# x^T U of the first two batches in plain float32: an attention and channel-mixing kernel on one core, with its steps in another order

## The chip, the cores and the metric

The kernel runs on one core of one Trainium2 chip. The metric is device time in microseconds: 933.13 us is the median of three runs of the kernel before (932.9 to 933.77). One profiled execution of it took 933.82 us; its trace spans 932.0 us. In the profile PE is TensorE (PEld its weight loads), DVE is VectorE, ACT is ScalarE, POOL is GpSimd and SP the engine that issues the transfers. A number like L449 is a line of the kernel.

## The reference

Linear attention with a norm for each head, then a low-rank mixing along the sequence and a feed-forward net, for 8 batches of 576 positions and 512 channels (8 heads of 64):

```python
kv = np.einsum('bhsd,bhse->bhde', k, v)
out = np.einsum('bhsd,bhde->bhse', q, kv)
rms = np.sqrt(np.mean(out * out, axis=-1, keepdims=True) + 1e-06)
x = (out / rms * g_norm)              # then heads side by side: [8, 576, 512]
...
xt = x.transpose(0, 2, 1)
h = xt @ U @ V                        # U: 576 x 32, V: 32 x 576
u = x + h.transpose(0, 2, 1)
ch = np.maximum(u @ w_ch1, 0.0) @ w_ch2   # 512 -> 2048 -> 512
y = u + ch
```

U, V and the two weights come as float64 bits, which the kernel turns into float32 on the chip with byte and bit operations.

## The kernel before, in words

**The feed-forward net** sets the frame. The 4608 rows (8 x 576) are cut into nine blocks of 512. For each block the 2048 hidden channels are taken in 16 chunks f of 128. A chunk is `ffn1` (L432 to L434: four column tiles d of 128 channels, three matmuls each), `relu` (ACT makes `hh`, L441, DVE makes `hl`, L442) and `ffn2` (L449: four output tiles, three matmuls each). The three matmuls are the two halves of a float32 split: a value is stored as a high part rounded to the type float32r and a low part, the rest, and high x high, low x high and high x low are added. So u is held as `uth` and `utl`, the hidden values as `hh` and `hl`, the weights as `ws` with two halves. `ffn2` of a chunk comes one chunk later, so that PE has `ffn1` of the next chunk to do while ACT and DVE make `hh` and `hl`.

**The preparation of a batch** goes in four pairs of heads. `kv` (L259, L263) makes the two 64x64 products into `kvb`; `out` (L282, L284) multiplies by q; ACT squares, DVE reduces (L298), ACT and DVE form the reciprocal root, DVE multiplies (L311, L313): x, with positions on partitions. Then x is split into `xh` (L142) and `xl` (L154, L327); `t_step` forms x^T U on PE with U in two parts (`u2`, 64 columns: high and low side by side; L354, L356), five matmuls with `xh` and four with `xl`; `t4_step` adds and splits the result into `t4`; `turn_step` transposes x on DVE (L339) and with 16 small transfers on SP (L342) into `ut32`; `mix_step` multiplies `t4` by V (L424), adds it to `ut32` (L426) and splits the sum into `uth` and `utl` (`split_cols`, L389, L390). From batch 2 on the last 64 positions of k and v are split too (`tails`, L254 to L256).

**Batch b+1 is prepared within block b.** A table, `STEPS`, gives the half chunk at which each pair's step is placed; batch 1 has its own, `STEPS0`, because block 0 also decodes the weights of its later chunks. The compiler's own scheduler may move an instruction from that place, by its model of time; what comes out is one fixed order on each engine.

**Batch 0 has nothing to hide behind.** Its steps, with the decoding of U, V and the first three chunks' weights, are named and listed by hand in `ORDER0`: `kv0`, `out0`, `sq0` (squares), `red0`, `ta0`/`hf0`/`rc0`/`nw0` (the root), `mul0`, `xh0`/`xl0`/`xt0` (the split of x), `tx0`/`txl0` (x^T U with the high and the low part of x: ten matmuls, L655, and four, L659), `t4c0`/`t4s0`, `tr0` (the transpose on PE, L650), `mix0` (L673), `uh0`/`ul0` (`uth` and `utl` of column tile 0), for pairs 0 to 3; `w1...`, `w2...`, `c...`, `e...` and `m...` are weights: A (copy of bytes, L128), D0 to D2 (DVE), B (merge, L129), H and L (the halves, L544 and L547). `f0a` to `f0d` are `ffn1` of chunk 0. The engines take their queues in that order. What of batch 0 does not fit in block 0, its last 64 positions, is done by `mix_rest` (L414, L416) at half steps 3, 5, 7 and 9 of block 0.

Slots of weights that come late serve as room for early data: `x123` (x of pairs 1 to 3) lies in weight 15's, `xhl0` (the split x of odd pairs) in 14's, `u4` (U in four parts) in 13's; a weight's load waits until its slot is free.

Of the kernel before, what the change touches and what calls it, by code (L numbers as in the profile page):

```python
# [58 lines left out]
def build(ctx: ExitStack, tc: tile.TileContext, kv_in, kvt0_in, kvt_in, q_in, uv_in, g_in, w_in, out):  # L59
# [285 lines left out]
    def t_step(b, p):  # L345
        xh, xl = state[b, p]["hl"]
        tp = bank()
        if b == 0:
            todo = [(u, xh, i) for u in u4 for i in range(NT)] + [(u4[0], xl, i) for i in range(4)]
            for n, (u, xx, i) in enumerate(todo):  # L350
                nc.tensor.matmul(tp[0:2 * R, 0:P], lhsT=u[:, i, :], rhs=xx[:, i, :], start=(n == 0), stop=(n == len(todo) - 1))
        else:
            for i in range(NT):
                nc.tensor.matmul(tp[0:2 * R, 0:P], lhsT=u2[:, i, :], rhs=xh[:, i, :], start=(i == 0), stop=(i == NT - 1))  # L354
                if i < 4:
                    nc.tensor.matmul(tp[0:2 * R, 0:P], lhsT=u2[:, i, :], rhs=xl[:, i, :], start=False, stop=False)  # L356
        state[b, p]["tp"] = tp

    def t4_step(b, p):
# [227 lines left out]
    step["u2v"] = lambda: nc.vector.tensor_copy(out=u2[:, :, 0:R], in_=u4[0][:, :, 0:R].bitcast(F32))  # L587
    step["u2a"] = lambda: nc.scalar.copy(out=u2[:, :, R:2 * R], in_=u4[1][:, :, 0:R].bitcast(F32))

    def first_pair(p):  # L590
# [16 lines left out]
        def kv():  # L607
# [29 lines left out]
        def x_high():  # L637
            own["xh"], own["xl"] = xhl0 if p % 2 else [sc.tile([P, n, P], F32R, name=s) for s, n in (("xh", NT), ("xl", 4))]
            nc.scalar.copy(out=own["xh"], in_=x)

        def x_low():
            nc.vector.tensor_tensor(out=own["xl"], in0=x[:, 0:4], in1=own["xh"][:, 0:4].bitcast(F32), op=ALU.subtract)

        def x_rest():
            xh = own["xh"]
            nc.vector.tensor_tensor(out=xh[TAIL:P, 4], in0=x[0:TAIL, 4], in1=xh[0:TAIL, 4].bitcast(F32), op=ALU.subtract)

# [8 lines left out]

        def t_low():
            for i in range(4):
                nc.tensor.matmul(tp, lhsT=u4[0][:, i, :], rhs=own["xl"][:, i, :], start=False, stop=(i == 3))  # L659
# [9 lines left out]
        def mix():  # L669
# [170 lines left out]
```

## Time and profile before

| | |
|---|---|
| median of 3 runs | 933.13 us (932.9 to 933.77) |
| the profiled execution | 933.82 us, its span 932.0 us |
| PE busy | 912.5 us, 98% of the span |
| DVE, ACT, POOL busy | 413.9, 280.5, 48.3 us |
| block 0, first FFN matmul | 30.30 us |
| block 1, first FFN matmul | 140.68 us |
| block 1, second chunk's first FFN matmul | 159.69 us |
| mean granted clock | 0.993 |

A busy PE may still be slow: the granted clock halves in some stretches, and a matmul's shown duration (0.39 us for 512 columns) is longer than its step from one to the next, since they overlap. So work is priced here by steps between starts.

### The profile page before, as it was taken

Reading aid. Unit: us, or ns where it says so; the run is one execution under the profiler, and the core shown is the slowest. Engines: PE = TensorE matmul, PEld = TensorE weight load, DVE = VectorE, ACT = ScalarE, POOL = GpSimd, SP = SyncE. Lnnn points to the kernel's source line nnn. Section 1 sums busy time; section 2 is a strip of 40 time slices with the busy share of each in tenths; the row PEclk is TensorE's granted clock in tenths of the full one; section 3 lists DMA queues with packets and bytes.
Section 4 is the critical chain, followed back from the end, with each engine's and each line's share of the span. In section 5 each row is a group of like instructions: output and inputs, shape, how many; then the busy total and the mean of one; then the engine's idle time right before and its main releaser. Section 6 shows DMA issues by size and latency. Waiting matters only on the chain.

```text
span 932.0 us, 12204 instructions
## 1 busy us (share of the span) xinstructions
PE 912.5 (98%) x4560; PEld 761.4 (82%) x4560; DVE 413.9 (44%) x890; ACT 280.5 (30%) x592; POOL 48.3 (5%) x66
## 2 busy tenths in 40 slices
PE   8899997999999999999999999999999999999998
PEld 7777886888888888888888888888788888888887
DVE  5889976444354345444244435434344331112112
ACT  6677753222223223222222222222222221111110
POOL 3000002000020002000200001000200020002000
PEclk9999997999999999999999999999999999999999
DMA  9951123321122121211122122212111010001001
GB/s 346 415 211 47 48 62 104 88 56 54 49 95 58 32 78 63 80 34 57 59 59 71 30 70 74 80 32 73 57 49 27 13 46 1 1 0 46 1 1 46
DMA packets 43019, 65.48 MB, mean 70 GB/s; under 512 B 9680, under 2 KB 27856, under 8 KB 42960
## 3 DMA queue, kind: packets, MB, share of 16 engines
q1 hardware_dynamic: 42960, 64.70, 21.2%
q8 instruction: 36, 0.59, 0.3%
q14 instruction: 23, 0.19, 0.1%
HBM read 46.97 MB, written 9.44 MB: 61 GB/s over the span
## 4 chain that ended last, share of the span: by engine, by line
PE 79%; DVE 1%; SPq 1%; DMA 1%; POOL 0%; issue 0%; DVEq 0%; POOLq 0%
PE y L449 36%; PE h L432 12%; PE h L433 12%; PE h L434 12%; PE pp L259 2%; PE pp L282 2%; SPq L342 1%; PE pp L354 1%; PE pp L449 1%; PE pp L356 1%; PE pp L424 1%; DVE utl L390 1%; PE pp L284 1%; DMA out<-st 0%; DVE st L460 0%; DMA kv_sb<-kv_in 0%
## 5 line engine op out<-in xcount | busy, mean ns | idle before, releaser
L449 PE MATMUL y<-hh,ws 128*128 128x512 f32 x1000 | 327.4, 394 | 2.9 <-ACT hh L441 2.9
L442 DVE SCALAR_TENSOR_TENSOR hl<-h,hh 128x512 fp32r<-128x512 f32 x143 | 98.6, 690 | 298.4 <-ACT hh L441 297.2
L449 PEld LDWEIGHTS y<-hh,ws 128*128 128x128 f32 x1000 | 180.8, 188 | 37.9 <-ACT hh L441 4.5
L441 ACT ACTIVATE hh<-h 128x512 fp32r<-128x512 f32 x143 | 85.3, 597 | 377.4 <-PE h L434 377.2
L432 PE MATMUL h<-uth,ws 128*128 128x512 f32 x500 | 197.1, 394 | 0.9 <-DVE hl L442 0.8
L433 PE MATMUL h<-utl,ws 128*128 128x512 f32 x500 | 195.3, 391 | 0.0
L434 PE MATMUL h<-uth,ws 128*128 128x512 f32 x500 | 194.9, 390 | 0.0
L449 PE MATMUL y<-hl,ws 128*128 128x512 f32 x500 | 193.6, 387 | 0.0
L432 PEld LDWEIGHTS h<-uth,ws 128*128 128x128 f32 x500 | 93.9, 188 | 22.4 <-DVE hl L442 2.2
L434 PEld LDWEIGHTS h<-uth,ws 128*128 128x128 f32 x500 | 93.9, 188 | 20.2
L449 PEld LDWEIGHTS y<-hl,ws 128*128 128x128 f32 x500 | 93.9, 188 | 19.4
L433 PEld LDWEIGHTS h<-utl,ws 128*128 128x128 f32 x500 | 94.0, 188 | 18.4
L461 POOL TENSOR_TENSOR st<-st,utl 128x512 f32<-128x512 f32 x32 | 41.1, 1304 | 791.4 <-DVE st L460 782.0
L449 PE MATMUL y<-hh,w2s 128*128 128x512 f32 (+1 forms) x144 | 47.9, 403 | 1.9 <-ACT w2s L544 1.2
L426 DVE TENSOR_TENSOR ut<-pp,ut 128x288 f32<-128x288 f32 x56 | 25.2, 457 | 54.9 <-DMA ut<-xt 29.9
L389 ACT ACTIVATE uth<-ut,g_sb 128x448 fp32r<-128x448 f32 (+7 forms) x56 | 27.6, 530 | 47.4 <-DVE ut L426 37.6
L460 DVE TENSOR_TENSOR st<-y,uth 128x512 f32<-128x512 f32 x32 | 21.2, 686 | 42.8 <-PE y L449 31.4
L449 PEld LDWEIGHTS y<-hh,w2s 128*128 128x128 f32 x144 | 27.4, 195 | 8.8 <-ACT hh L441 1.7
L282 PE MATMUL pp<-kvb,q_sb 128*128 128x128 f32 x224 | 30.5, 280 | 2.8 <-DVE kvb L270 2.8
L298 DVE TENSOR_REDUCE sums<-x 128x10 f32<-128x640 f32 x28 | 22.9, 818 | 23.0 <-ACT x L286 22.9
L390 DVE SCALAR_TENSOR_TENSOR utl<-ut,g_sb,uth 128x448 fp32r<-128x448 f32 (+7 forms) x56 | 26.9, 513 | 13.1 <-ACT uth L389 8.0
L259 PE MATMUL pp<-kv_sb 128*128 128x128 f32 x224 | 31.4, 281 | 0.4 <-DMA kv_sb<-kv_in 0.4
(199 smaller groups left out, 881.3 us busy)
## 6 DMA issues: line engine op xcount, KB each, us to landing
kv_sb<-kv_in SPq DMA_DIRECT2D x29, 512.0 KB, 3.6
raw<-w_in SPq DMA_DIRECT2D x14, 1023.6 KB, 15.3
q_sb<-q_in SPq DMA_DIRECT2D x29, 288.0 KB, 2.9
out<-st SPq DMA_DIRECT2D x32, 256.0 KB, 2.0
ut<-xt SPq DMA_DIRECT2D x224, 20.0 KB, 1.8
ut<-xt SPq DMA_DIRECT2D x224, 16.0 KB, 1.8
kvt_sb<-kvt_in SPq DMA_DIRECT2D x27, 128.0 KB, 3.2
kvq<-kv_in SPq DMA_DIRECT2D x3, 512.0 KB, 8.2
```

The lines of the kernel that those rows point to most:

```text
L259: nc.tensor.matmul(pp[:, 0:P], lhsT=m[:, i * P:(i + 1) * P], rhs=m[:, MAIN + i * P:MAIN + (i + 1) * P], start=(i == 0 and b < NATIVE), sto ...
L282: nc.tensor.matmul(big[:, i * P:(i + 1) * P], lhsT=qt[:, TAIL + i * P:TAIL + (i + 1) * P], rhs=kb, start=True, stop=True)
L389: nc.scalar.mul(out=hi, in_=src, mul=g_sb)
L390: nc.vector.scalar_tensor_tensor(out=lo, in0=src, scalar=g_sb, in1=hi.bitcast(F32), op0=ALU.mult, op1=ALU.subtract)
L426: nc.vector.tensor_tensor(out=own, in0=mp, in1=own, op=ALU.add)
L432: nc.tensor.matmul(h, lhsT=w1s[f][0][:, d, :], rhs=uh[:, d, :], start=(d == 0), stop=False)
L433: nc.tensor.matmul(h, lhsT=w1s[f][0][:, d, :], rhs=ul[:, d, :], start=False, stop=False)
L434: nc.tensor.matmul(h, lhsT=w1s[f][1][:, d, :], rhs=uh[:, d, :], start=False, stop=(d == ND - 1))
L441: last["relu"] = nc.scalar.activation(out=hh, in_=h, func=AF.Relu)
L442: nc.vector.scalar_tensor_tensor(out=hl, in0=h, scalar=0.0, in1=hh.bitcast(F32), op0=ALU.max, op1=ALU.subtract)
L449: nc.tensor.matmul(acc, lhsT=w2s[f][w][:, c, :], rhs=h[:, cols], start=(f == 0 and w == 0 and h is hh), stop=(f == NF - 1 and w == 1))
L461: nc.gpsimd.tensor_tensor(out=o, in0=o, in1=ul[:, c, :].bitcast(F32), op=ALU.add)
```

## The change

In batches 0 and 1 (`b < NATIVE`), x^T U is done with plain float32 matmuls: five for a pair, with x as it stands and U as it stands (`uf`, written twice side by side, so that the result has the 64 rows that `t4` needs). `xh`, `xl`, the four parts of U and their steps are gone for these batches, and `t4` of batch 1 is made as batch 0's is, with one copy and one subtraction. `u2`, which batches 2 to 7 still use, is made later from `uf` (`u2h`, `u2l`, at the list's end). The slots of weights 13 and 14 no longer hold early data. `ORDER0` is written anew. `STEPS0` puts batch 1's kv at half step 2, out at 3, t at 8 and mix at 9, and five half steps apart from pair to pair, where it was 3, 4, 9, 10 and six. Line numbers of the new kernel are lower by about ten from L490 on (L655 becomes L634, L650 L630, L673 L648; L259 becomes L261, L282 L284, L441 stays).

```diff
-STEPS0 = dict(kv=3, out=4, t=9, mix=10, gap=6)
+STEPS0 = dict(kv=2, out=3, t=8, mix=9, gap=5)
...
+    uf = const.tile([P, NT, 2 * R], F32, name="uf")
...
     def xsplit_step(b, p):
 
         s = state[b, p]
-        if b == 0 and p % 2 == 1:
-            xh, xl = xhl0
-        else:
-            xh = sc.tile([P, NT, P], F32R, name="xh")
-            xl = sc.tile([P, 4, P], F32R, name="xl")
-        n = p if b == 0 else -1
+        if b < NATIVE:
+            return
+        xh = sc.tile([P, NT, P], F32R, name="xh")
+        xl = sc.tile([P, 4, P], F32R, name="xl")
+        n = -1
...
     def t_step(b, p):
-        xh, xl = state[b, p]["hl"]
         tp = bank()
-        if b == 0:
-            todo = [(u, xh, i) for u in u4 for i in range(NT)] + [(u4[0], xl, i) for i in range(4)]
-            for n, (u, xx, i) in enumerate(todo):
-                nc.tensor.matmul(tp[0:2 * R, 0:P], lhsT=u[:, i, :], rhs=xx[:, i, :], start=(n == 0), stop=(n == len(todo) - 1))
-        else:
+        if b < NATIVE:
+            for i in range(NT):
+                nc.tensor.matmul(tp[0:2 * R, 0:P], lhsT=uf[:, i, :], rhs=state[b, p]["x"][:, i, :], start=(i == 0), stop=(i == NT - 1))
+        else:
+            xh, xl = state[b, p]["hl"]
...
-        if b == 0:
-            move("t4", p, t4[0:2 * R], tp[0:2 * R, 0:P])
+        if b < NATIVE:
+            move("t4", p if b == 0 else 0, t4[0:2 * R], tp[0:2 * R, 0:P])
...
-    xhl = weight_slot("xhl0", [P, NT + 4, P], F32R, 14)
...
-    u4t = weight_slot("u4", [P, 2, NT, 2 * R], F32R, 13)
...
-    step["u4h"] = lambda: nc.scalar.copy(out=h4, in_=uv4)
-    step["u4l"] = lambda: nc.gpsimd.tensor_tensor(out=l4, in0=uv4, in1=h4.bitcast(F32), op=ALU.subtract)
+    step["u4h"] = lambda: nc.scalar.copy(out=uf.rearrange("p i (n r) -> p i n r", n=2), in_=uv4)
...
+    step["u2h"] = lambda: nc.scalar.copy(out=u2[:, :, 0:R], in_=uf[:, :, 0:R])
+    step["u2l"] = lambda: nc.vector.tensor_tensor(out=u2[:, :, R:2 * R], in0=uf[:, :, 0:R], in1=u2[:, :, 0:R].bitcast(F32),
+                                                  op=ALU.subtract)
...
-        def t_high():
-            for n, u in enumerate(u4):
-                for i in range(NT):
-                    nc.tensor.matmul(tp, lhsT=u[:, i, :], rhs=own["xh"][:, i, :], start=(n + i == 0), stop=False)
-
-        def t_low():
-            for i in range(4):
-                nc.tensor.matmul(tp, lhsT=u4[0][:, i, :], rhs=own["xl"][:, i, :], start=False, stop=(i == 3))
+        def t():
+            for i in range(NT):
+                nc.tensor.matmul(tp, lhsT=uf[:, i, :], rhs=x[:, i, :], start=(i == 0), stop=(i == NT - 1))
```

Three places in the engines' orders carry the prediction.

First, PE at the end of batch 0 and the start of block 0. Before, with L655 and L659 the last pair's x^T U, L259 and L263 the kv step of batch 1's first pair, and L432 the first FFN matmul:

```order
L655 MATMUL pp<-xhl_126,u_147 64x128 x10
L259 MATMUL pp<-kv_sb 128x128 x4
L263 MATMUL pp<-kvt_sb 128x128
L659 MATMUL pp<-xhl_126,u_147 64x128 x4
L673 MATMUL y<-v_97,st 128x4x64 x2
L432 MATMUL h<-uth,w1s_347 128x512
L433 MATMUL h<-utl,w1s_347 128x512
```

In the new kernel, where L634 is x^T U and L261 and L265 are the kv step:

```order
L634 MATMUL pp<-x_126,uf 64x128 x5
L648 MATMUL y<-v_98,st 128x4x64 x2
L630 MATMUL y<-ident,x_126 128x128 x4
L432 MATMUL h<-uth,w1s_322 128x512
L261 MATMUL pp<-kv_sb 128x128 x4
L414 MATMUL pp<-ident,x 128x64
L416 MATMUL pp<-v_98,t_345 128x64
L265 MATMUL pp<-kvt_sb 128x128
L433 MATMUL h<-utl,w1s_322 128x512
```

The kv step of batch 1 and the first `mix_rest` (L414, L416; it stood further ahead before) have moved from before the first FFN matmul to behind it.

Second, ACT around the first two relus of block 0 (L441). Before, with L129 the merge and L128 the byte copy of a weight, L544 the cast to a high half:

```order
L129 COPY top<-temps 128x512
L441 ACTIVATE hh<-h 128x512
L544 CAST w2s_489<-temps 128x512
...
L544 CAST w2s_507<-dec 128x512
L129 COPY top<-dec 128x1024
L441 ACTIVATE hh<-h 128x512
L144 ACTIVATE ut_0_89<-pp,g_sb 128x64
L142 COPY kvb_98<-pp 64x64 x2
L128 COPY dec<-raw_175 128x1024
```

In the new kernel (L131 the merge, L130 the byte copy, L536 the cast):

```order
L536 CAST w2s_420<-temps 128x512
L441 ACTIVATE hh<-h 128x512
L131 COPY top<-dec 128x512 x2
L536 CAST w1s_441<-dec 128x512
L536 CAST w2s_447<-dec 128x512
L131 COPY top<-dec 128x1024
L130 COPY dec<-raw_170 128x1024
L441 ACTIVATE hh<-h 128x512
L144 COPY kvb_99<-pp 64x64 x2
```

The cast of w2 for chunk 0 now stands ahead of the first relu, and a byte copy for weight 3 ahead of the second.

Third, PE where block 1 begins: its first L432 to L434 take `uth` and `utl` of one column tile after the other. Before, L424 is the mix of batch 1's pair 3, L257 to L284 are batch 2:

```order
L354 MATMUL pp<-xh,u_96 64x128
L432 MATMUL h<-uth,w1s_347 128x512
...
L424 MATMUL pp<-v_97,t_1406 128x288 x2
L257 MATMUL pp<-tails 128x256
L259 MATMUL pp<-kv_sb 128x128 x4
L282 MATMUL pp<-kvb_98,q_sb 128x128 x4
L284 MATMUL pp<-kvb_98,q_sb 128x128
...
L434 MATMUL h<-uth,w1s_347 128x512
...
L449 MATMUL y<-hh,w2s_489 128x512 x4
```

The L434 shown is the last of the fourth tile; the other three tiles stand ahead of L424. In the new kernel L424 of pair 3 of batch 1 stands 80 rows further ahead, and the one here is batch 2's:

```order
L424 MATMUL pp<-v_98,t_1217 128x288 x2
...
L449 MATMUL y<-hh,ws_1276 128x512 x4
L432 MATMUL h<-uth,w1s_322 128x512
...
L424 MATMUL pp<-v_98,t_1618 128x288 x2
L284 MATMUL pp<-kvb_100,q_sb 128x128 x4
L449 MATMUL y<-hh,w2s_420 128x512
L432 MATMUL h<-uth,w1s_441 128x512
```

All four tiles of the first chunk stand together now; of batch 2, the kv steps (L259, L261) have gone ahead into block 0.

More of the change, by code (lines that the diff above doesn't have):

```diff
@@ L498, in build @@
         nc.gpsimd.memset(t[:, 0:1].bitcast(F32), 0.0)
-    for t in xhl0:
-        nc.gpsimd.memset(t[:, 0, 0:1].bitcast(F32), 0.0)
-    u4t = weight_slot("u4", [P, 2, NT, 2 * R], F32R, 13)
-    u4 = [u4t[:, n] for n in range(2)]
-    for t in u4:
-        nc.gpsimd.memset(t[:, 0, 0:1].bitcast(F32), 0.0)
     uvs = weight_slot("uvs", [P, DM], I64, 12)
@@ L586, in build @@
     step["v4g"] = lambda: [spread_v(n, nc.gpsimd.tensor_copy) for n in (1, 2, 3)]
-    step["u2v"] = lambda: nc.vector.tensor_copy(out=u2[:, :, 0:R], in_=u4[0][:, :, 0:R].bitcast(F32))
-    step["u2a"] = lambda: nc.scalar.copy(out=u2[:, :, R:2 * R], in_=u4[1][:, :, 0:R].bitcast(F32))
+    step["u2h"] = lambda: nc.scalar.copy(out=u2[:, :, 0:R], in_=uf[:, :, 0:R])
+    step["u2l"] = lambda: nc.vector.tensor_tensor(out=u2[:, :, R:2 * R], in0=uf[:, :, 0:R], in1=u2[:, :, 0:R].bitcast(F32),
+                                                  op=ALU.subtract)
     def first_pair(p):
-        m, t, qt = loads.pop(("kv", 0, p)), loads.pop(("t", 0, p)), loads.pop(("q", 0, p))
+        m, kt, qt = loads.pop(("kv", 0, p)), loads.pop(("t", 0, p)), loads.pop(("q", 0, p))
         at = 2 * P * (p // 2)
@@ L610, in kv @@
                                  start=(i == 0), stop=False)
-            nc.tensor.matmul(kv_ps, lhsT=t[half:half + TAIL, 0:P], rhs=t[half:half + TAIL, P:2 * P], start=False, stop=True)
+            nc.tensor.matmul(kv_ps, lhsT=kt[half:half + TAIL, 0:P], rhs=kt[half:half + TAIL, P:2 * P], start=False, stop=True)
         def kv_copy():
@@ L635, in mul @@
                                     in1=rv[0:TAIL, 4].unsqueeze(2).broadcast_to([TAIL, 2, D]), op=ALU.mult)
[L637 to L646, printed above, removed]
         def turn():
@@ L675, in first_pair @@
         steps = dict(
-            kv=kv, kvb=kv_copy, out=out, sq=squares, nw=newton, mul=mul, xh=x_high, xl=x_low, xt=x_rest, tr=turn,
-            tx=t_high, txl=t_low, t4c=t4_high, t4s=t4_low, mix=mix,
+            kv=kv, kvb=kv_copy, out=out, sq=squares, nw=newton, mul=mul, tr=turn,
+            tx=t, t4c=t4_high, t4s=t4_low, mix=mix,
             red=lambda: nc.vector.tensor_reduce(out=sums.rearrange("p (i h) -> p i h", h=2), in_=xv, axis=AX.X, op=ALU.add),
```

13 lines of the change are left out of this document (6 added, 7 removed).

## The prediction

> **What bounds the kernel now.** I read the page's busy shares and slices first, then who PE waited for, then PE's timeline wherever a wait showed, and last the other engines at those places.
>
> ```profile
> PE   8899997999999999999999999999999999999998
> PEclk9999997999999999999999999999999999999999
> ...
> PE pp L282 <- DVE kvb L270: 2.8, 1, 2.8
> ```
>
> PE is busy nearly everywhere, so time is PE's work plus what PE loses by waiting or by a lower clock. The losses are in the first two slices (of 23.3 us each) and in the seventh, 140 to 163 us, the one with a lower granted clock. The list of PE's waits names the longest single one, 2.8 us for `kvb`. Two windows size them; the first runs from block 0's first FFN matmul to block 1's first, the second from there to block 1's second chunk (a chunk is one f: 12 matmuls of L432 to L434 and 12 of L449):
>
> ```profile
> 30.30:140.68 110.38, 104.72 (x502) 83.59 (x500) 94.47 (x182) 76.09 (x118) 0.00 (x0) 0.98 0.38 139
> 140.68:159.69 19.01, 13.90 (x67) 11.47 (x65) 13.10 (x29) 6.25 (x17) 5.51 (x4) 0.73 0.36 119
> ```
>
> The columns are length, then busy time of PE, PEld, DVE, ACT and POOL, then the granted clock. The second window is 19 us long, for one chunk, at clock 0.73. PE's timeline there:
>
> ```profile
> 140.68 0.44 PE L432 MATMUL h<-uth,w1s 128*128 128x512 f32 x1
> ...
> 144.99 1.05 PE L259 MATMUL pp<-kv_sb 128*128 128x128 f32 x8
> 148.81 2.08 PE L282 MATMUL pp<-kvb,q_sb 128*128 128x128 f32 x8 [2.76 <-DVE kvb L270]
> ...
> 153.22 0.55 PE L257 MATMUL pp<-tails 128*128 128x256 f32 x1 [1.91 <-DVE r L301]
> 153.83 0.80 PE L432 MATMUL h<-uth,w1s 128*128 128x512 f32 x1
> 155.01 0.80 PE L433 MATMUL h<-utl,w1s 128*128 128x512 f32 x1 [0.38 <-DVE utl L390]
> ...
> 159.69 0.50 PE L432 MATMUL h<-uth,w1s 128*128 128x512 f32 x1
> ```
>
> Three of the four column tiles of block 1 are ready at 140.68. The fourth, batch 1's last pair, enters at 153.83. Between them PE took up batch 2's steps in its order, and these waited too. Why the fourth is late is seen on SP and DVE:
>
> ```profile
> 137.71 10.62 SPq L342 DMA_DIRECT2D ut<-xt  x16
> ...
> 133.23 0.29 DVE L255 TENSOR_TENSOR tails<-kvt_sb,tails 64x128 fp32r<-64x128 f32 x1
> ...
> 145.72 1.26 DVE L255 TENSOR_TENSOR tails<-kvt_sb,tails 64x128 fp32r<-64x128 f32 x1
> 147.00 1.26 DVE L256 TENSOR_TENSOR tails<-kvt_sb,tails 128x128 fp32r<-128x128 f32 x1
> 148.17 0.58 DVE L270 TENSOR_REDUCE kvb<-pp 64x64 f32<-64x128 f32 x2
> 152.62 0.46 DVE L426 TENSOR_TENSOR ut<-pp,ut 128x288 f32<-128x288 f32 x1
> 154.27 0.68 DVE L390 SCALAR_TENSOR_TENSOR utl<-ut,g_sb,uth 128x448 fp32r<-128x448 f32 x1
> ```
>
> Pair 3's sixteen transposing transfers are issued from 137.71 to 148.33, so its second half can be added (L426) only after that; in DVE's order it stands behind batch 2's tails, L270 and more, and comes at 152.62. The split (L390) follows, and PE's L433 waits for it. The fourth tile was due nine FFN matmuls after 140.68 and comes 11 us later. What PE had to do in the window: 24 FFN matmuls at 0.228 (below) 5.5, eight float32 matmuls of L259 and five of L282/L284 at 0.235 3.0, and L424, L257 and one set of nine t matmuls 1.0 (an estimate from their columns): 9.5 us in all. So **9.5 us are lost here**; the window's row bounds it, from 5.1 (19.01 less 13.90 busy) to 10.2 (that and 27% of 19.01 by the clock).
>
> **The change part by part.** Prices first:
>
> ```profile
> 18.70 1.11 PE L619 MATMUL y<-kvb,kvq 128*128 128x128 f32 x8
> 19.64 0.39 PE L620 MATMUL pp<-kvb,kvq 128*128 128x128 f32 x2
> ...
> 140.20 0.23 PE L356 MATMUL pp<-xl,u 128*64 128x128 f32 x1
> ...
> 140.62 0.22 PE L354 MATMUL pp<-xh,u 128*64 128x128 f32 x1
> ...
> 46.02 0.43 PE L414 MATMUL pp<-ident,x 64*128 64x64 f32 x2
> 46.38 0.30 PE L416 MATMUL pp<-v,st 128*128 128x64 f32 x1
> ...
> L142 ACT CAST xh<-x 128x640 fp32r<-128x640 f32 x2 | 1.5, 732 | 1.3 <-DVE x L313 1.3
> L154 DVE TENSOR_TENSOR xl<-x,xh 128x512 fp32r<-128x512 f32 x2 | 1.3, 666 | 0.0
> ```
>
> Four plain float32 matmuls of 128 columns take 0.94 from start to start, 0.235 each (two records each); seven steps between the two rows of t take 0.42, 0.06 each. No row shows float32 with 64 weight columns. Below, it could be half of 0.235 if the weights set the pace, 0.12; above, the 0.36 of L414, the dearest float32 step shown. I take 0.235, since moving columns and type are those of L619.
>
> *Batch 1's t.* Nine at 0.06 (0.54) become five at 0.235 (1.18): +0.64 a pair, **+2.5** for four, all on PE, which is the bound (from +0.2 to +5.0).
>
> *The splits dropped in batch 1*, 0.73 of ACT and 0.67 of DVE a pair with a smaller correction, lie beside PE's matmuls, so I cost their removal at nothing; DVE (94.47 busy of 110.38 in block 0) gets some 3 us of slack. The two copies that now make u2 lie in block 0's first chunks, and batch 2's first t is a block away; without that cover PE would wait for both.
>
> *Transfers.*
>
> ```profile
> raw<-w_in SPq DMA_DIRECT2D x14, 1023.6 KB, 15.3
> ```
>
> The freed slots let weights 13 and 14, 1 MB each, be issued before weights 10 to 12 and batch 1's second kv, which so land 5 us later (2 MB at the 418 GB/s of the window from 30 to 40 us, below). That kv is issued once pair 0's kv step is done, near 30; with the 15.3 of a weight in this queue and the 5 it lands at 50. Its use is at half step 7, in chunk 3; chunk 1 begins at 40.20 and two chunks of FFN matmuls take 11, so not before 51. Nothing, and up to 2 if the queue is slower. Weight 15 now waits on SP for the x slot with pair 1's transposes behind it; the slot is freed by the tail mix of pair 3 at half step 9, and those transposes belong to a mix at half step 14. Nothing.
>
> *Start of block 0 and its first chunks*:
>
> ```profile
> 28.27 1.10 PE L259 MATMUL pp<-kv_sb 128*128 128x128 f32 x8
> ...
> 29.72 0.46 PE L659 MATMUL pp<-xhl,u 128*64 128x128 f32 x4
> ...
> 30.30 0.40 PE L432 MATMUL h<-uth,w1s 128*128 128x512 f32 x1
> ...
> 33.88 0.50 PE L433 MATMUL h<-utl,w1s 128*128 128x512 f32 x1 [0.51 <-DVE utl L683]
> ...
> 35.80 2.07 PE L449 MATMUL y<-hh,w2s 128*128 128x512 f32 x4 [1.19 <-ACT w2s L544]
> ...
> 40.20 0.40 PE L432 MATMUL h<-uth,w1s 128*128 128x512 f32 x1
> ...
> 42.71 0.39 PE L434 MATMUL h<-uth,w1s 128*128 128x512 f32 x1
> ...
> 43.78 1.20 PE L449 MATMUL y<-hh,w2s 128*128 128x512 f32 x4 [0.69 <-ACT hh L441]
> ...
> 41.78 1.35 ACT L129 COPY top<-dec 128x1024 uint8<-128x1024 uint8 x1
> 44.26 1.13 ACT L128 COPY dec<-raw 128x1024 uint8<-128x1024 uint8 x1
> ...
> 30.00:40.00 10.00, 8.20 (x31) 5.90 (x30) 8.68 (x23) 5.67 (x9) 0.00 (x0) 0.83 1.01 418
> ```
>
> An FFN matmul takes 0.228 (eleven steps from 40.20 to 42.71). Ahead of block 0's first FFN matmul PE drops 56 t matmuls at 0.06 (3.4) and gets 20 at 0.235 (4.7); the kv step of batch 1 (1.45, from 28.27 to 29.72) and one tail mix (0.5) now stand behind it. That is +1.3 − 1.95; DVE's splits are gone from the last pair's chain, and its longer t stands on it. I take **−0.7** at 30.30 (from −2.0, PE's share alone with t free, to +0.8, if none of the moved work had been on the path), and **+1.95** in block 0.
>
> Chunk 0 took 9.90 (to 40.20) for 5.8 of work: PE waited 0.51 for the last `utl`, then 1.19 for the w2 cast, and then ran slowly: the window's clock of 0.83 is 1.7 us lost, 3.4 at half speed. In the new order of ACT that cast stands ahead of the first relu, so PE waits about 1.2 for the relu alone: 4.1 lost become 1.2, **−2.9**. In its place comes one in chunk 1: ACT now has the 1.13 `raw` copy of another chunk between the 1.35 merge and the second relu, where before it came after (44.26). The relu is then 1.1 late and PE, which was held 0.69 there, 1.8; with such a half-clock stretch behind it at even odds (1.7) that is +1.1 + 0.85 = **+1.9**. Queued behind the relu are DVE's `hl` and PE's eight matmuls on it. Of the waits in the chunks after it, the one before chunk 5's L449,
>
> ```profile
> 74.68 1.21 PE L449 MATMUL y<-hh,ws 128*128 128x512 f32 x4 [1.54 <-ACT hh L441]
> ```
>
> finds a less loaded ACT: −1.5; in chunks 2 to 4 and later an `hl` behind decode steps on DVE is late by as much: +1.1. Together **−0.4**.
>
> The clock: half speed came after a stretch with waits of 0.5 and 1.19, and not after the single 1.54, so the limit lies near what chunk 1 will show; hence even odds. [...]
>
> *The boundary.* With five half steps a pair, pair 3's out step moves from half step 22 to 18 and its mix from 28 to 24, two chunks (11 us of FFN matmuls alone) earlier. In PE's old order that mix (L424) stands behind block 1's first three tiles, in the new one about three chunks ahead of its first, so SP's sixteen transfers and DVE's part end well before. All four tiles of block 1's first chunk then stand together, and of batch 2 only L424 and L284 remain inside it (1.3 of the 4.0). So the 9.5 lost fall to 0.5 (0 to 9.5), **−9.0**, and 2.7 of work moves into block 0, which changes nothing in sum.
>
> Against the profiled execution: start 30.3 − 0.7 = 29.6; block 0 110.4 + 2.5 + 1.95 + 2.7 − 2.9 + 1.9 − 0.4 = 116.15; the first chunk of block 1 19.0 − 9.0 − 2.7 = 7.3; the rest, 159.69 to 932.0, 772.3 as it is. **Span 925.4**, 6.6 less. The profiled execution took 933.82 for its span of 932.0; the median of the runs is 933.13, so I forecast 933.1 − 6.6 = **926.5**.
>
> **The rivals.** *More is gained.* Float32 t at 64 columns costs 0.12 (−2.3), chunk 1 keeps the full clock (−0.85), and the late relu is partly covered by DVE (−1.0): 922.3. For it: the stationary side is half as wide as L619's. Against: the moving side is the same. Chance 0.15.
>
> *The early chunks cool the array.* Chunks 1 to 3 have waits of 1.1 to 2.1 each; if each is followed by a half-clock stretch, 1.7 apiece, that is 5.1 − 0.85 more, 930.8, and with t at 0.36 (+2.5) 933.3, no change. For it: the clock of 0.83 from 30 to 40. Against: the 0.69 and 1.54 waits at 43.78 and 74.68 did not lower it. Chance 0.11.
>
> *The boundary stall stays*, and it is slower. The wait named there, 2.76, is for batch 2's own kvb, behind tails that took 1.26 each where 0.29 is usual (133.23), with POOL adding `st` beside them: if finishing block 0 slows DVE again and it is this, not batch 1's lateness, that stops PE, the 9.0 stay and t's cost remains: 926.5 + 9.0 = 935.5. It decides as soon as more than 7 of the 9.5 stay. Against it: these tails and L270 now stand before DVE's first L460, in the new order. [...] Chance 0.07.
>
> **How the numbers follow.** The forecast has 0.67. A measurement of this kernel tells 0.2%, 1.9 us, from no change. Its own range is 923.5 to 929.5 (t's 64-column price, one half-clock stretch more or less, the start's ±1.2); to leave out no more than two in ten I go from 921.5 to 931.5, which takes in the first rival and most of the second. Faster: 0.67 + 0.15 and a few of the second, 0.85; the rest of the second is no change, 0.07; slower, the third with the second's far end, 0.08.
>
> **What would show it.** Right: L350 of the new kernel at about 1.2 a pair; the window from block 1's first chunk to its second at 6 to 8 us and clock 1.00; block 0 longer than before, by about 6; the first FFN matmul at 29 to 30. Wrong: a wait of over 2 us near 145; the clock at 0.50 in more than one stretch between 35 and 60; the rest after the boundary differing from 772 by more than 1.5.

## The result, and the profile after

The changed kernel takes **925.67 us** (median; 924.8 to 926.72) where the kernel before, on the same chip, takes 933.01 (931.99 to 933.77): ratio 0.9922, 95% interval 0.9905 to 0.994. The forecast was 926.5, in a range from 921.5 to 931.5. The profiled execution took 925.85 us for a span of 924.0. Beside three of the experiments it came out once more, at 925.28 against 932.32 (0.9923, 0.991 to 0.9937). Kernels of different groups of runs are compared below by their ratio to the kernel before on their own chip; one per mille is 0.93 us.

The busy shares and two of the rows in 40 slices, from the page of the changed kernel:

```profile
PE 910.9 (99%) x4548; PEld 761.0 (82%) x4548; DVE 402.2 (44%) x870; ACT 271.4 (29%) x572; POOL 47.8 (5%) x61
...
PE   8899999999999999999999999999999999999998
...
PEclk9999999999999999999999999999999999999999
```

The seventh slice, which had a 7 in both rows, has a 9. The two windows of the prediction, block 0 and block 1's first chunk, in the changed kernel (length, busy PE, PEld, DVE, ACT, POOL, clock, DMA share, GB/s):

```profile
29.95:145.50 115.55, 111.06 (x558) 90.58 (x557) 96.66 (x191) 73.17 (x115) 0.00 (x0) 1.00 0.40 147
145.50:151.44 5.94, 5.94 (x32) 5.10 (x31) 2.82 (x6) 1.31 (x4) 1.67 (x2) 1.00 0.34 113
```

So the second window fell from 19.01 to 5.94, with no idle time and the full clock; block 0 is 5.17 longer; it begins 0.35 earlier; and what comes after 151.44 lasts 772.56 where it was 772.3. The sum is −0.35 + 5.17 − 13.07 + 0.25 = −8.0, the difference of the spans. Timeline of the changed kernel's PE and SP (SPq: the queue of SP's own DMA issues) at the places that the prediction named:

```profile
36.20 1.19 PE L449 MATMUL y<-hh,w2s 128*128 128x512 f32 x4 [0.69 <-ACT hh L441]
...
44.12 1.20 PE L449 MATMUL y<-hh,w2s 128*128 128x512 f32 x4 [1.69 <-ACT hh L441]
...
66.69 1.31 PE L350 MATMUL pp<-x,uf 128*64 128x128 f32 x10
67.93 1.20 PE L449 MATMUL y<-hh,ws 128*128 128x512 f32 x4
...
118.24 10.01 SPq L343 DMA_DIRECT2D ut<-xt  x16
...
150.06 0.42 PE L424 MATMUL pp<-v,t 128*128 128x288 f32 x2
150.32 1.05 PE L284 MATMUL pp<-kvb,q_sb 128*128 128x128 f32 x8
...
151.44 0.40 PE L432 MATMUL h<-uth,w1s 128*128 128x512 f32 x1
```

Pair 3's sixteen transposing transfers are issued by 128.25, 17 us ahead of block 1, where before they ran until 148.33, 8 us into it. Five float32 t matmuls take 1.24 us from start to start (66.69 to 67.93), 0.248 each. The two waits in chunks 0 and 1 are the forecast 1.2 and 1.8 in kind (0.69 and 1.69, both for ACT's relu), but neither is followed by a lower clock (1.00 over block 0's window).

### The profile page after: what moved, and what is told of

Its sections match the earlier page's. It is cut to its first block, busy times and chain, and to the rows that moved or that the text cites. A ratio compares the mean times of both kernels' runs of the same rounds, so it can differ in the third digit from the quotient of the medians.

```text
span 924.0 us, 12146 instructions
## 1 busy us (share of the span) xinstructions
PE 910.9 (99%) x4548; PEld 761.0 (82%) x4548; DVE 402.2 (44%) x870; ACT 271.4 (29%) x572; POOL 47.8 (5%) x61
## 4 chain that ended last, share of the span: by engine, by line
PE 86%; DVE 6%; DMA 3%; ACT 2%; SPq 2%; issue 1%; POOL 0%; DVEq 0%; POOLq 0%; ACTq 0%
PE y L449 37%; PE h L432 13%; PE h L433 13%; PE h L434 13%; PE pp L261 2%; PE pp L284 2%; SPq L343 2%; DVE dec L127 1%; DVE st L460 1%; DMA kvq<-kv_in 1%; ACT top L131 1%; DMA out<-st 1%; DVE hl L442 1%; PE pp L354 1%; PE pp L424 1%
## 5 line engine op out<-in xcount | busy, mean ns | idle before, releaser
L449 PE MATMUL y<-hh,ws 128*128 128x512 f32 x1000 | 328.1, 394 | 0.0
L449 PEld LDWEIGHTS y<-hh,ws 128*128 128x128 f32 x1000 | 181.0, 189 | 33.1 <-issue 0.2
L441 ACT ACTIVATE hh<-h 128x512 fp32r<-128x512 f32 x143 | 85.4, 597 | 404.0 <-PE h L434 404.0
L432 PE MATMUL h<-uth,ws 128*128 128x512 f32 x500 | 197.5, 395 | 2.2 <-DVE hl L442 2.2
L434 PE MATMUL h<-uth,ws 128*128 128x512 f32 x500 | 195.1, 390 | 0.0
L449 PE MATMUL y<-hl,ws 128*128 128x512 f32 x500 | 193.6, 387 | 0.0
L432 PEld LDWEIGHTS h<-uth,ws 128*128 128x128 f32 x500 | 93.9, 188 | 24.9 <-DVE hl L442 4.3
L434 PEld LDWEIGHTS h<-uth,ws 128*128 128x128 f32 x500 | 93.9, 188 | 20.2
L449 PEld LDWEIGHTS y<-hl,ws 128*128 128x128 f32 x500 | 93.9, 188 | 19.2
L449 PE MATMUL y<-hh,w2s 128*128 128x512 f32 (+1 forms) x144 | 48.1, 396 | 2.8 <-ACT hh L441 2.7
L426 DVE TENSOR_TENSOR ut<-pp,ut 128x288 f32<-128x288 f32 x56 | 25.0, 455 | 43.5 <-DMA ut<-xt 30.3
L449 PEld LDWEIGHTS y<-hh,w2s 128*128 128x128 f32 x144 | 26.6, 188 | 10.1 <-ACT hh L441 4.6
L261 PE MATMUL pp<-kv_sb 128*128 128x128 f32 x224 | 30.3, 275 | 0.0
L284 PE MATMUL pp<-kvb,q_sb 128*128 128x128 f32 x224 | 29.5, 275 | 0.0
```

The lines of the kernel that those rows point to most:

```text
L261: nc.tensor.matmul(pp[:, 0:P], lhsT=m[:, i * P:(i + 1) * P], rhs=m[:, MAIN + i * P:MAIN + (i + 1) * P], start=(i == 0 and b < NATIVE), sto ...
L284: nc.tensor.matmul(big[:, i * P:(i + 1) * P], lhsT=qt[:, TAIL + i * P:TAIL + (i + 1) * P], rhs=kb, start=True, stop=True)
L432: nc.tensor.matmul(h, lhsT=w1s[f][0][:, d, :], rhs=uh[:, d, :], start=(d == 0), stop=False)
L434: nc.tensor.matmul(h, lhsT=w1s[f][1][:, d, :], rhs=uh[:, d, :], start=False, stop=(d == ND - 1))
L441: last["relu"] = nc.scalar.activation(out=hh, in_=h, func=AF.Relu)
L449: nc.tensor.matmul(acc, lhsT=w2s[f][w][:, c, :], rhs=h[:, cols], start=(f == 0 and w == 0 and h is hh), stop=(f == NF - 1 and w == 1))
```

## The experiments

Three questions were put: whether the half steps are what cleared the boundary, whether each term of block 0's sum has its price, and what the half clock costs. Two kernels that do one part of the change each, one that undoes one part, and the changed kernel itself ran on one chip.

**The half steps alone.** The kernel before with

```diff
-STEPS0 = dict(kv=3, out=4, t=9, mix=10, gap=6)
+STEPS0 = dict(kv=2, out=3, t=8, mix=9, gap=5)
```

> The kernel before with one line changed: batch 1's half steps of the change (kv 2, out 3, t 8, mix 9, five a pair); x and U keep their high and low parts in both batches and the written order of block 0's start is the old one. Theory of the prediction: the steps alone take batch 1's last pair off block 1's first chunk, so the window from block 1's first FFN matmul to its second chunk falls from 19.0 to 6 to 7.5 us, while the 2.5 us of float32 t in batch 1 and the changes at the start are not paid: 933 - 9 = about 924 us, and down to 922 if some of the stall's half clock goes with it. Rival: the steps are not enough, because pair 3's split of x and its two corrections lengthen its chain and it is still late at the boundary: the window stays above 12 us and the time at 927 to 933 us.

Measured: 922.54 us, ratio 0.9891 (0.9878 to 0.9905). Its windows for block 0, the first chunk of block 1, and block 0's start up to its third chunk:

```profile
30.77:143.12 112.35, 108.05 (x532) 87.27 (x531) 101.40 (x205) 80.14 (x130) 0.00 (x0) 0.98 0.40 147
143.12:148.54 5.42, 5.42 (x32) 4.47 (x31) 1.93 (x4) 0.69 (x2) 1.06 (x1) 1.00 0.12 28
30.77:48.93 18.16, 15.66 (x66) 11.75 (x64) 15.53 (x34) 12.17 (x21) 0.00 (x0) 0.91 1.01 419
```

The boundary is as short as in the changed kernel, with the splits of x and U all in place. Block 0 grows by 1.97, less than the 2.7 of batch-2 work that I had moved into it. In the third window the clock of 0.91 is the half-clock stretch that the kernel before has there too in its first profile (0.91 from 30.30 to 48.42). This one line is faster than the whole change by 2.7 us.

**Everything but the half steps.** The changed kernel with the STEPS0 of before.

> The changed kernel with batch 1's old half steps (kv 3, out 4, t 9, mix 10, six a pair); float32 t and the new start stay. Theory of the prediction: the half steps are what cleared the boundary, so most of the 9.5 us lost there is back: window from block 1's first FFN matmul to its second chunk 15 to 19 us, time 930 to 935 us. Rival: the shorter chain of a pair (no split of x, t straight from x) lets pair 3's transposing transfers start a half chunk earlier, and POOL and DVE are less loaded; then the stall is mostly gone with the old steps too: window 6 to 9 us, time 923 to 926 us, the same as the changed kernel. In that case either part would have done it.

Measured: 929.4 us, 0.9964 (0.9951 to 0.9976). Windows, and SP's row for pair 3's transfers, of this kernel:

```profile
30.08:147.56 117.48, 112.99 (x538) 90.38 (x537) 92.62 (x177) 71.55 (x109) 0.00 (x0) 0.97 0.38 139
147.56:156.37 8.81, 7.43 (x43) 5.87 (x41) 8.07 (x15) 2.38 (x6) 4.21 (x3) 1.00 0.29 100
53.25:60.07 6.82, 6.82 (x17) 4.98 (x17) 6.53 (x17) 4.25 (x9) 0.00 (x0) 0.50 0.30 120
```
```profile
132.78 10.01 SPq L343 DMA_DIRECT2D ut<-xt  x16
```

The boundary window is 8.81, not the 15 to 19 that my theory gave: 10.2 of the 13.1 us are gone without the half steps (in both figures 2.5 to 3, by PE's records, is work of batch 2 that has gone ahead into block 0). The transfers now begin at 132.78 and not at 137.71, while block 1 begins 6.9 later, so they end 4.8 us ahead of it. On the boundary the rival was right: either part alone does most of it, and the two do not add. On the time it was wrong (923 to 926), since block 0 is 7.1 us longer than before; 3.4 of that is half clock, from 53.25 to 60.07, after a wait of 1.92 us for the relu in chunk 2.

**Batch 1's split put back.** The changed kernel with `b < NATIVE` made `b < 1` in `xsplit_step`, `t_step` and `t4_step`.

> The changed kernel with the split of x, the nine float32r matmuls of t and their t4 steps put back in batch 1 alone; batch 0, the half steps and the start stay. Theory of the prediction: PE is the bound in block 0, so its 4 x 0.64 = 2.5 us of extra t work comes off: 925.7 - 2.5 = about 923.2 us, if the 2.9 us of ACT and 2.7 us of DVE that come back lie beside PE's matmuls as I priced them (nothing). Rival: they do not, and PE's waits for the relu and for hl in the chunks of block 0 grow by as much as its work shrinks: 925 to 926.5 us, no difference from the changed kernel.

> The changed kernel itself beside the other three on the same chip, as what they are compared with: 925.7 us (925 to 926.7).

Measured: 924.77 us, 0.9917 (0.9905 to 0.9929), beside 925.28, 0.9923 (0.991 to 0.9937) for the changed kernel: no difference that can be told, and nearer the rival's forecast than the theory's. Windows of the first, then of the second:

```profile
30.12:145.49 115.37, 109.35 (x547) 87.89 (x545) 100.71 (x202) 78.56 (x129) 0.00 (x0) 1.00 0.40 146
145.49:150.91 5.42, 5.42 (x32) 4.48 (x31) 1.93 (x4) 0.69 (x2) 1.06 (x1) 1.00 0.12 29
```
```profile
29.73:145.22 115.49, 111.08 (x559) 90.53 (x558) 96.72 (x191) 73.11 (x115) 0.00 (x0) 1.00 0.40 147
145.22:151.16 5.94, 5.94 (x33) 5.09 (x32) 2.83 (x6) 1.31 (x4) 1.68 (x2) 1.00 0.33 113
```

PE is busy 1.73 less in block 0 and idle 1.61 more (115.37 − 109.35 against 115.49 − 111.08). The new idle time, from the timeline with the split put back:

```profile
75.59 1.19 PE L449 MATMUL y<-hh,ws 128*128 128x512 f32 x4 [0.38 <-ACT hh L441]
...
77.26 0.50 PE L432 MATMUL h<-uth,ws 128*128 128x512 f32 x1 [0.20 <-DVE hl L442]
...
118.04 0.27 PE L354 MATMUL pp<-xh,u 128*64 128x128 f32 x1 [0.23 <-ACT xh L144]
118.75 0.50 PE L432 MATMUL h<-uth,ws 128*128 128x512 f32 x1 [0.44 <-DVE hl L442]
...
125.51 0.50 PE L432 MATMUL h<-uth,ws 128*128 128x512 f32 x1 [0.50 <-DVE hl L442]
```

These make 1.75 us; behind chunk 4 of the changed kernel there is one such wait, of 0.21. Over all of block 0 behind chunk 1 the waits that the timelines show come to 3.65 us with the split and to 2.11 without it. So the split work of ACT and DVE, which I had priced at nothing, costs here most of what float32 t costs.

**Float32 t in batch 1 without the new start.** The fourth corner of the square: new half steps, batch 0 as before, and

```diff
+    uf = const.tile([P, NT, 2 * R], F32, name="uf")
...
+        if b == 1:
+            for i in range(NT):
+                nc.tensor.matmul(tp[0:2 * R, 0:P], lhsT=uf[:, i, :], rhs=state[b, p]["x"][:, i, :], start=(i == 0), stop=(i == NT - 1))
```

> The new half steps for batch 1 as in e1, and float32 t in batch 1 alone: x unsplit and U plain there, batch 0 and the written order of its start as before (one copy of U to a float32 tile is added at the end of that order). With e1, e3 and the changed kernel it makes a square: t split or float32 in batch 1, by old or new start. Theory of the prediction (t costs 0.64 us a pair on PE, the dropped splits save nothing): e1 and 2.5 us, 925.0 us, ratio to before 0.992. Rival, from e3, where putting the split back gained only about 0.5 us: the splits that are dropped save PE's waits for the relu and hl in block 0, nearly as much as t costs: 922.5 to 923.3 us, ratio 0.9895 to 0.9903; then the 2.7 us by which the changed kernel is behind e1 lie in batch 0's part, the new start.

Measured: 925.8 us, 0.9923 (0.991 to 0.9937). Windows:

```profile
30.56:145.39 114.83, 110.43 (x555) 89.72 (x553) 97.80 (x196) 76.06 (x120) 0.00 (x0) 1.00 0.41 148
145.39:150.38 4.99, 4.99 (x25) 4.17 (x24) 1.62 (x3) 0.64 (x2) 0.75 (x1) 1.00 0.25 96
```

By its time the rival fell: against the half steps alone this kernel takes 3.3 us more. But that is not the price of t alone, which by the steps is 2.8 (twenty matmuls at 0.248 less 36 at 0.06). Block 0 is 2.48 longer, and the two windows do not hold the same work: here a mix and most of an out step of batch 2 stand ahead of block 1 (143.31 to 144.38, 1.07 us) and eight more of its t matmuls (0.5 us). PE's waits in block 0 behind chunk 1 fall from 1.71 us (0.69, 0.55, 0.20 and 0.27, with the half steps alone) to a single 0.69, so the splits that are dropped do give back 1.0 us there. And what comes behind block 1's first chunk is 1.96 longer (773.82 against 771.86), with a stall of its own in it (SP, DVE and PE of this kernel; L435 is the mix's addition, L426 before):

```profile
157.43 16.89 SPq L346 DMA_DIRECT2D ut<-xt  x20
```
```profile
163.07 0.46 DVE L435 TENSOR_TENSOR ut<-pp,ut 128x288 f32<-128x288 f32 x1 [3.95 <-DMA ut<-xt]
...
164.91 0.50 PE L441 MATMUL h<-uth,ws 128*128 128x512 f32 x1 [1.04 <-DVE hl L451]
```

DVE stands still for 3.95 us until batch 2's transposing transfers have landed, which SP issues from 157.43 on, behind block 0's output; `hl` stands behind that addition in DVE's order, and PE waits 1.04 for it. In the changed kernel the same addition waits 0.54. So the square does not give two prices that add: float32 t in batch 1 costs 3.2 per mille with the old start and 0.6 with the new one, and some 2 us of that difference lie behind the boundary, in the order of this one kernel.

**Is it DVE's load or ACT's?** Batch 1's split as above, with its subtraction (DVE, 0.67 a pair) on POOL, and in a second kernel its copy (ACT, 0.73 a pair) on POOL:

```diff
-        minus("xl", n, xl, s["x"][:, 0:4], xh[:, 0:4].bitcast(F32))
+        low = nc.gpsimd if b == 1 else nc.vector
+        low.tensor_tensor(out=xl, in0=s["x"][:, 0:4], in1=xh[:, 0:4].bitcast(F32), op=ALU.subtract)
```

> e3 (the changed kernel with t split again in batch 1) with the subtraction that makes the low part of x in batch 1, 0.67 us a pair on DVE, given to POOL, which has nothing to do in block 0. It asks whether DVE's load is what cost e3 the 2.0 us that it should have gained: PE in e3 waits 1.1 us more for hl (DVE) and 0.4 more for hh (ACT) in the chunks after chunk 4. If DVE's load is the cause: DVE 2.7 us less, the waits for hl near 118 and 125 us gone, 923.0 to 924.0 us, ratio to before 0.990 to 0.991. If it is not (the waits come from ACT, or POOL's reads slow DVE by as much): no gain, 924.5 to 926 us, ratio 0.9915 to 0.993.

> e3 with the copy that makes the high part of x in batch 1, 0.73 us a pair on ACT, given to POOL instead; the subtraction stays on DVE. If ACT's load is what cost e3 its gain: ACT 2.9 us less, the wait for hh near 75.6 us and the wait for xh near 118 us gone, 923.0 to 924.0 us, ratio 0.990 to 0.991. If not: no gain, 924.5 to 926 us, ratio 0.9915 to 0.993, with the waits for hl still there.

Measured: 923.43 us, 0.9903 (0.9888 to 0.9918), and 923.92 us, 0.9908 (0.9892 to 0.9925), where the split without POOL has 0.9917. From the groups of POOL in the first, and PE's timeline in the second:

```profile
L328 POOL TENSOR_TENSOR xl<-x,xh 128x512 fp32r<-128x512 f32 x4 | 7.9, 1983 | 99.8 <-ACT xh L144 42.8 <-ACT uth L136 38.6 <-PE pp L425 18.3
```
```profile
124.67 0.50 PE L435 MATMUL h<-uth,ws 128*128 128x512 f32 x1 [1.27 <-DVE hl L445]
```

Both medians lie in the range of "this load is the cause", 1.3 and 0.85 us under the split without POOL, but both intervals overlap its interval. In the first the waits for `hl` behind chunk 4 fall to one of 0.39, and a wait for the relu of 0.69 appears: 1.08 in all, where the split without POOL has 1.75. In the second the wait for the relu at 75 us, which should have gone, is still there (0.38), with 0.20 and the 1.27 shown for `hl`: 1.85 in all, no less. So PE's waits bear out DVE's load and not ACT's, and the times alone settle neither.

**Twice the t.** The changed kernel with batch 1's five t matmuls done twice.

```diff
-            for i in range(NT):
+            for i in [*range(NT)] * (1 + b):
```

> The changed kernel with batch 1's ten float32 records of t issued twice (each pair's t adds the same five matmuls again, so batch 1's t is doubled): 20 float32 matmuls of 128 columns more in block 0, at 0.248 each by the changed kernel's trace 4.96 us of PE. It asks whether PE's time in block 0 counts in full there, since e9 lost 2.5 us of block 0 to float32 t and e3 gained only 0.1 by taking it out. Theory of the prediction (PE is the bound): block 0 longer by 5.0 us, time 930.3 us, ratio to before 0.9975. Rival, from e3: DVE and ACT pace block 0 in the changed kernel, so a part of it lies in PE's waits: 926 to 928.5 us, block 0 longer by 1 to 3 us.

Measured: 931.37 us, 0.9973 (0.9962 to 0.9985), which is 5.0 per mille or 4.7 us over the changed kernel for 4.96 us of matmuls. Windows:

```profile
29.62:152.13 122.51, 118.18 (x608) 97.03 (x607) 97.74 (x193) 74.15 (x118) 0.00 (x0) 0.99 0.40 145
152.13:157.12 4.99, 4.99 (x24) 4.17 (x23) 1.61 (x3) 0.63 (x2) 0.75 (x1) 1.00 0.00 0
54.50:58.50 4.00, 3.74 (x10) 2.98 (x11) 3.93 (x8) 1.52 (x2) 0.00 (x0) 0.57 0.35 119
```

Block 0 grows by 7.0, of which 0.95 was moved over the boundary and 1.7 is a half-clock stretch of this execution. Five of the seven executions, this one among them, show a mean clock of 0.997 or 0.998; the two at 1.000 took 929.89 and 930.55, 3.4 and 4.0 us over what the changed kernel's ratio gives on this chip (926.5). So most of PE's added time counts in the changed kernel, more than the rival's 1 to 3, and PE is the bound there when work is added. When work is taken from PE and put on ACT and DVE, as the split does, PE waits for them instead.

**What stopped PE at the boundary.** The kernel before, with POOL's addition of `ul` left out in block 0's finish.

> The kernel before without POOL's addition of the low part of u to block 0's result, so that block 0's output lacks it; nothing else changes. It asks what stopped PE at the boundary. Theory of the prediction: batch 1's last pair is late there whatever POOL does, since its transfers are issued until 148.3; DVE's two tails of 1.26 us beside POOL's addition fall to 0.29 each, so kvb comes some 2 us earlier, but the fourth tile does not: window from block 1's first FFN matmul to its second chunk 16.5 to 19 us, time 930.5 to 933 us. Rival of the prediction: the slowed tails are the cause; the stall falls by 7 us or more: window under 12 us, time 926 us or less.

Measured: 933.02 us, 1.0 (0.9991 to 1.001). Its window, and DVE's and PE's rows:

```profile
140.30:159.06 18.76, 13.80 (x67) 10.80 (x65) 12.11 (x32) 6.38 (x17) 0.00 (x0) 0.77 0.41 126
```
```profile
145.34 0.29 DVE L255 TENSOR_TENSOR tails<-kvt_sb,tails 64x128 fp32r<-64x128 f32 x1
145.64 0.29 DVE L256 TENSOR_TENSOR tails<-kvt_sb,tails 128x128 fp32r<-128x128 f32 x1
...
146.49 1.16 PE L282 MATMUL pp<-kvb,q_sb 128*128 128x128 f32 x8 [0.82 <-DVE kvb L270]
...
150.73 0.80 PE L432 MATMUL h<-uth,w1s 128*128 128x512 f32 x1 [0.23 <-ACT uth L389]
...
154.41 2.07 PE L259 MATMUL pp<-kv_sb 128*128 128x128 f32 x8 [1.29 <-DMA kv_sb<-kv_in]
```

The tails take 0.29 and not 1.26, and the wait for `kvb` is 0.82 and not 2.76, yet the window is 18.76 and the time is the same. To take away most of the longest wait of the list bought nothing. The fourth tile did come sooner, which I had ruled out: 10.4 us after block 1's first matmul (150.73), where it was 13.2. It is still far behind the nine matmuls ahead of it (2.05), since pair 3's transfers are issued until 148.04 here too, and PE loses the 2.7 us again behind it, 1.29 of them in a wait for batch 2's k and v. So POOL's addition lengthens the last pair's lateness and does not make it. That the lateness is what costs the time is shown by the half steps alone, which take the pair away from there.

**The half clock in chunk 0.** First, the half steps alone with five matmuls that fill chunk 0's wait:

```diff
+                for _ in range(5):
+                    nc.tensor.matmul(y[0][2], lhsT=w1s[0][0][:, 0, :], rhs=ut[0][1][:, ND - 1, :], start=True, stop=True)
```

> e1 (new half steps alone) with five FFN-sized matmuls more, whose result is overwritten, in front of chunk 0's first L449: they fill the 1.19 us in which PE there waits for the w2 cast, and leave the rest as it is. Theory of the prediction: that wait, on top of the 0.51 ahead of it, is what halves the clock for the following 3.4 us, so with PE kept busy the half clock is gone and 1.7 us with it: e1 less 1.7, about 920.8 us (ratio to before 0.9873), chunk 0 in 8.2 us where e1 has 9.95. Rival: the clock follows something else than these waits (PE's total use in the start), the stretch stays or comes later: 922.5 us, ratio 0.989, chunk 0 at 9.9 us.

Measured: 922.29 us, 0.9884 (0.9871 to 0.9898), not told apart from 0.9891. Its window from block 0's first FFN matmul to its third chunk, and PE's wait in chunk 1:

```profile
30.83:48.80 17.97, 15.57 (x70) 11.46 (x69) 15.55 (x34) 12.01 (x21) 0.00 (x0) 1.00 1.01 418
```
```profile
44.15 1.21 PE L449 MATMUL y<-hh,w2s 128*128 128x512 f32 x4 [1.47 <-ACT hh L441]
```

The half clock is gone and chunk 0 took 8.38 where it took 9.95, but chunk 1 took 9.59 where it took 8.21: PE only waits longer for the relu. Then the kernel before itself, profiled once more:

> The kernel before once more, for a second look at chunk 0 of block 0. In two kernels with the same waits there (0.52 and 1.19 us) the clock was halved for 3.4 us and in two others it was not, and in all of them chunk 1's first L449 came about 13.4 us after block 0's first FFN matmul. If the half clock is a matter of the single execution, this profile may show chunk 0 at 8.4 us and a wait of 1.5 us in chunk 1 in place of 9.9 and 0.7, with chunk 2 starting at the same time after block 0's start (18.1 us); if it belongs to the kernel, chunk 0 takes 9.9 us again. The boundary is expected as before: window from block 1's first FFN matmul to its second chunk 18.5 to 19.5 us.

Its windows, and below them the same stretch of the first profile of the kernel before:

```profile
29.93:47.87 17.94, 14.36 (x65) 10.54 (x64) 15.48 (x34) 11.35 (x19) 0.00 (x0) 1.00 1.01 419
140.05:158.13 18.08, 12.62 (x66) 10.20 (x64) 13.08 (x29) 6.38 (x18) 5.51 (x4) 0.81 0.37 125
```
```profile
30.30:48.42 18.12, 15.63 (x65) 11.79 (x64) 15.47 (x34) 11.51 (x19) 0.00 (x0) 0.91 1.01 419
```

The boundary's 18.08 is a little under what was expected, with a clock of 0.81 there for 0.73. In chunk 0 the same kernel with the same waits of 0.51 and 1.19 kept its full clock this time (1.00 where it was 0.91), and reached its third chunk only 0.18 us sooner. So this stretch is a matter of the single execution (what decides it, no run shows), and worth 0.2 us and not 1.7: ACT's decoding sets when chunk 1's L449 begins.

**The raw copy behind the relu.** The changed kernel with

```diff
-                    with tc.issue_after(done["ul3"].ins):
+                    with tc.issue_after(last["relu"].ins if f == 1 else done["ul3"].ins):
```

and this loop moved behind the chunk's relu.

> The changed kernel with the decoding of the weights two chunks ahead issued behind the second chunk's relu where it was issued ahead of it, so that the 1.1 us raw copy stands behind that relu on ACT as it did before the change. Theory of the prediction (its term for chunk 1): PE's wait ahead of chunk 1's first L449 falls from 1.7 to 0.7 us and the time by 1.0, to about 924.5 us (ratio 0.9915 where the changed kernel has 0.9923). Rival: the copy is only late somewhere else, and a later chunk waits for its weights or relu by as much: 925.3 to 926 us, chunk 1 shorter by 1 and a later chunk longer by 1.

Measured: 927.2 us, 0.9942 (0.993 to 0.9955), outside both forecasts, and slower than the changed kernel by the medians, though the two intervals overlap. PE's timeline, and one window:

```profile
43.26 0.96 PE L449 MATMUL y<-hh,w2s 128*128 128x512 f32 x3 [0.69 <-ACT hh L441]
...
76.56 1.20 PE L449 MATMUL y<-hh,ws 128*128 128x512 f32 x4 [1.28 <-ACT hh L441]
77.74 0.40 PE L424 MATMUL pp<-v,t 128*128 128x288 f32 x1
78.34 0.77 PE L432 MATMUL h<-uth,ws 128*128 128x512 f32 x1 [0.20 <-DVE hl L442]
```
```profile
78.30:81.70 3.40, 3.36 (x8) 2.69 (x9) 3.40 (x11) 2.17 (x3) 0.00 (x0) 0.51 0.00 0
```

The wait in chunk 1 did fall from 1.69 to 0.69, as forecast; a new one of 1.28 stands in chunk 5, with a half-clock stretch behind it. That stretch takes 1.7 of the 3.2 us by which block 0 grew (118.69); where the rest went the trace does not say in one place. Two of the five executions show a mean clock of 0.998, the profiled one among them, and took 928.93 and 928.46; the three at 1.000 took 926.4 to 927.2. So such a stretch costs about its 1.7 in this kernel, where in chunk 0 it cost 0.2.

## Why the prediction was right, point by point

*The boundary* (−9.0, and 2.7 moved into block 0: −11.7; measured −13.07). The mechanism stands: the last pair of batch 1 was late. The half steps alone clear it, and without POOL's addition the time stays. The longest wait on the profile's list named a victim, and the prediction was right to ask which pair was late. It was wrong, though, to give the whole gain to the half steps: the rest of the change, with its shorter chain of a pair, takes 10.2 off the window without them.

*Float32 t* (+0.235 each, +2.5): right. 0.248 each by the trace, which makes 2.8; for twenty matmuls more (4.96) the time rises by 3.4 to 4.7. The rival at 0.12 is out.

*The splits dropped in batch 1, at nothing*: this is the step that was mis-sized. PE's waits in block 0 behind chunk 1 fall by 1.0 us when they are dropped with the old start (1.71 to 0.69) and by 1.5 with the new one (3.65 to 2.11). I had weighed DVE's share of block 0 (94.47 of 110.38) as slack, and did not ask in which chunks it was short. The sum hardly shows this, because part of the saving stood in it under another name: the −1.5 for the wait ahead of chunk 5's L449, with ACT less loaded, in the term of −0.4. That wait is gone in the changed kernel. The waits behind chunk 1 were 2.92 before (0.69, 0.69, 1.54) and are 2.12 (0.97, 0.94, 0.21): −0.8 for the forecast −0.4.

*Chunks 0 and 1*: the total was right and its reading was not, so that it came out is luck. The forecast for both with the moved kv step was −2.9 + 1.9 + 1.95 = +0.95; block 0's third chunk began 18.12 after the first FFN matmul and now begins 18.81 after (29.95 to 48.76), +0.7. But I counted half clock as lost in chunk 0 (−1.7 when gone) and at even odds in chunk 1 (+0.85). The runs show one thing in place of these: PE reaches chunk 1's L449 early or late and waits there for ACT, so what it loses in chunk 0 is covered, all but 0.2 us.

*Start* (−0.7, measured −0.35, and −0.2 from the second profile of before to the second of the changed kernel), *the rest* (772.3, measured 772.56 and 771.94) and *the transfers* (nothing; no wait of PE for a transfer in block 0) held.

*Rivals.* The cooling of the early chunks did not come in either profile of the changed kernel, though 1.69, 0.97 and 0.94 us of waits were there; but two of its nine executions show a mean clock of 0.998, and took 926.7 and 926.6, some 1.4 us more than the other seven, and the kernel with t doubled had such a stretch in its profile (clock 0.57 from 54.50 to 58.50), with waits of 0.95 and 0.92 that ended at 52.20 and 54.76. So this rival may have come in those two executions, at an estimated one stretch each (1.7 us of the 1.8 that a mean clock of 0.998 takes from 924); where it fell in them is not on record. The stall that stays fell with POOL's addition left out: the window kept 18.76 us, though DVE's tails took 0.29 in place of 1.26.

What stays open is why float32 t in batch 1 takes 3.3 us more with the old start and 0.5 with the new one. Some 2 us of the difference lie behind block 1's first chunk, where the kernel with the old start and float32 t waits for batch 2's transfers; no run changes that order alone. Open too is why PE waits more behind chunk 1 with the new start than with the old, with the split (3.65 and 1.71) and without it (2.11 and 0.69). The order in which the scheduler lays the decoding among the chunks may be the reason, but no run here isolates it.

## What to carry to other kernels

When two edits could each remove the same stall, run each alone: here one line of half steps gave 922.5 us, and the rest of the change gave back 2.7 of it. Before work on another engine is priced at zero, ask in which chunk that engine is short, not how busy it is over the block. Before the growth of a window is called a price, count whether it still holds the same work: the scheduler moves steps across its ends. And before counting a lost stretch as gain, look at who sets the next wait: the half clock ahead of a wait for ACT was worth 0.2 us of the 1.7 that it took from PE.

## What the runs showed of the hardware

The granted clock was 0.50 in some stretches. In the first profile of the kernel before these are two, from 35.75 to 39.16 in chunk 0 of block 0 and from 148.39 to 158.63 at the boundary; between them and after the second the clock is 1.00. Length, busy PE, PEld, DVE, ACT and POOL, clock, DMA share and GB/s:

```profile
35.75:39.16 3.41, 3.36 (x8) 2.68 (x9) 3.06 (x9) 1.58 (x4) 0.00 (x0) 0.50 1.01 420
148.39:158.63 10.24, 7.47 (x25) 6.12 (x26) 6.63 (x19) 4.70 (x12) 1.73 (x1) 0.50 0.57 199
```

With the old steps it was 0.50 from 53.25 to 60.07, with the raw copy moved 0.51 from 78.30 to 81.70, and with t twice 0.57 from 54.50 to 58.50. Each of these had waits of PE ahead of it or at its start: 0.51 and 1.19 in chunk 0, 2.76 at the boundary, 1.92 with the old steps, 1.28 and 0.20 with the raw copy moved, 0.95 and 0.92 with t twice. But such waits did not always bring it. The second profile of the kernel before has the same 0.51 and 1.19 in chunk 0 at a clock of 1.00, and the changed kernel has 1.69, 0.97 and 0.94 at 1.00. What decides between the two, these runs do not show.

In batch 1's split POOL took 1.98 us for a subtraction of 128x512 that DVE does in 0.67 in the kernel before, and 0.94 for a copy of 128x640 that ACT does there in 0.73.
